# Attention and gated feed-forward in one kernel: values loaded in 128-token chunks and spread on chip, a mask by matmul in the first unit, and a new order in units 0 to 2

## The chip, the cores and the metric

The kernel runs on one core of a Trainium2 chip. The core has a matrix engine (TensorE, PE in the profile), a vector engine (VectorE, DVE), an activation engine (ScalarE, ACT), GpSimd (POOL), which here mostly issues loads, and SyncE (SP), which issues the stores of the output. Each engine runs its own instructions in program order and waits on semaphores for the others. The metric is the device time of one execution in microseconds, the median of several runs.

## The reference

There are 4 batches of 8 heads, 768 tokens, 64 numbers per head. Each query looks at the tokens less than 16 away and, through one summary key and value per block of 32 tokens, at all 24 blocks. The summary key is the maximum over the block, the summary value is its mean, and log(32) is added to the summary scores. A feed-forward stage follows:

```python
mask_l = np.abs(pos[:, None] - pos[None, :]) < window
scores_s = scale * einsum('bhsd,bhnd->bhsn', q, k_sum) + np.log(block)
a = softmax(concatenate([where(mask_l, scores_l, -1e9), scores_s]))
x = matmul(a, concatenate([v, v_sum]))          # to [3072, 512]
ffn_out = (gelu(x @ w_gate) * (x @ w_val)) @ w_out
return x + sigmoid(x @ w_res) * ffn_out
```

All inputs and the output are float32; the kernel computes in bf16 with float32 sums.

## The kernel before, in words

A unit is half a batch, 384 tokens, so there are 8 units. Within a unit the attention works in tiles of 64 queries (`QT`), six per unit, and by head pairs, four of them. The whole kernel is written out by hand under `tc.manual_schedule()`: the order of the source is the order on each engine.

**Keys.** `load_tokens` brings keys and queries to `k_sb` and `q_sb` (96 rows of consecutive tokens). `k_step` turns one head pair on PE (`turn_pair`, L204), lets ACT copy it (L211) into `kW`, lets DVE take the maximum over each block of 32 (L214) and copies the 16 neighbours on either side and the 24 block keys next to every tile (L218 to L220). So each 64-query tile has one stationary operand of 128 columns: 96 band keys and 24 block keys.

**Values.** `vext` holds for each of the 12 tiles of a batch 128 rows: 96 band values (a tile's own 64 and 16 on each side) and the block values. The band rows come straight from memory, so that tokens near a tile's border are loaded twice: by `v_tile` (L95, one tile, 8 heads) or, for tiles 1 to 5 of batch 0, by `v_head` (L101). In addition, the second half of each batch is loaded densely to `v_sb`. The block means are matmuls: `vsum_dense` and `vsum_pair` for batch 0; `vsum_grp` (L250, three groups side by side) and `vsum_place` (L257) for the others. `vsum_bc` (L263, DVE) copies the means to the last 32 rows of every tile of `vext`.

**Attention of a unit.** `s_step` computes the scores of a head pair (L273), ACT takes the exponential (L277), and DVE multiplies by the band mask (L280). `av_step` multiplies by `vext` (L296); the last column of `vext` is 1, so that it yields the denominators; DVE divides (L304, L306). `xt_step` turns the result for the feed-forward (L315, L317).

**Feed-forward of a unit.** Twelve `fo_step`s: gate and value matmuls (L328, four each), Gelu on ACT (L334), product on DVE (L335). The accumulators come from a ring of four PSUM buffers (`ps_mm`), two steps' worth. Then `res_step`, `ffn_step` and `end_step` for three groups of 128 tokens, with the attention of the next unit placed among them: this is the tail of the unit.

**Order of the work.** Before the loop over the units stands the start: keys and queries of batch 0, attention of unit 0, the first gate and value products. `turn_pair` work for the next batch stands among the `fo_step`s of the odd units; in unit 1 from step 2, in units 3 and 5 from step 0. All loads are issued by POOL in program order: keys and queries of batch 0, values, gate and value weights, `w_res`, `w_out`, then `load_batch(1)`, `load_batch(2)`, `load_batch(3)`. At most eight are in flight: each waits for the one eight places before it.

```python
def half_fo(st, w, fo, lo, hi, acc=None): acc = ps_mm.tile(...)   # L323, ring of 4
i = fo - (2 if u == 1 else 0)                                      # L420
k_step(nb, hp, *home) / q_step(q_sb[nb], nb, 0, S, hp, *home)      # L428, L430
load_batch(1)                                                      # L401
```

Of the kernel before, what the change touches and what calls it, by code (L numbers as in the profile page):

```python
# [8 lines left out]
F32 = mybir.dt.float32  # L9
# [6 lines left out]
def kernel(  # L16
# [45 lines left out]
    OWN, POST, BLK0 = WIN, WIN + QT, BAND  # L62
# [4 lines left out]
    bmat = const.tile([BAND, HT, 32], BF16, name="bmat")  # L67
    bden = const.tile([PP, 44], BF16, name="bden")
# [5 lines left out]
    place = const.tile([PP, 32], BF16, name="place")  # L74
    vpart = const.tile([128, DM], BF16, name="vpart")
# [16 lines left out]
    def v_tile(b, t):  # L92
        lo, hi = max(0, t * QT - WIN), min(S, t * QT + QT + WIN)
        r0 = lo - (t * QT - WIN)
        nc.gpsimd.dma_start(out=vext[b % 2][r0:r0 + hi - lo, t, :, 0:D],  # L95
                            in_=v[b, :, lo:hi, :].rearrange("h p d -> p h d"))

    def v_head(b, h, t0, t1):
        src = bass.AP(tensor=v.tensor, offset=v[b, h, t0 * QT - WIN:, :].offset,
                      ap=[[D, BAND], [QT * D, t1 - t0], [1, D]])  # L100
        nc.gpsimd.dma_start(out=vext[b % 2][0:BAND, t0:t1, h, 0:D], in_=src)  # L101

    k_sb, q_sb, v_sb = {}, {}, {}

    with tc.manual_schedule():

        def vext_consts(i):
            nc.vector.memset(vext[i][:, :, :, D:D + 1], 1.0)
            nc.vector.memset(vext[i][0:32, 0, :, 0:D], 0.0)
            nc.vector.memset(vext[i][64:96, NT - 1, :, 0:D], 0.0)  # L110

        def vext_edges(i):
            nc.gpsimd.affine_select(out=vext[i][0:32, 0, :, D:D + 1], in_=vext[i][0:32, 0, :, D:D + 1],
                                    compare_op=ALU.is_ge, fill=0.0, base=-WIN,
                                    pattern=[[0, H], [0, 1]], channel_multiplier=1)
            nc.gpsimd.affine_select(out=vext[i][64:96, NT - 1, :, D:D + 1],
                                    in_=vext[i][64:96, NT - 1, :, D:D + 1],
                                    compare_op=ALU.is_ge, fill=0.0, base=WIN - 1,
                                    pattern=[[0, H], [0, 1]], channel_multiplier=-1)

        def kw_consts(i):
            for p in range(NP):
                nc.vector.memset(kW[i][p][:, 0, 0:WIN], 0.0)
                nc.vector.memset(kW[i][p][:, NT - 1, POST:POST + WIN], 0.0)
                nc.vector.memset(kW[i][p][:, :, BLK0 + NB:128], 0.0)

        def own_rows(base, row, tile, block):
            nc.gpsimd.affine_select(out=bmat[:], in_=bmat[:], compare_op=ALU.is_ge, fill=0.0, base=base,
                                    pattern=[[tile, HT], [block, 32]], channel_multiplier=row)
# [4 lines left out]

        nc.vector.memset(ident[:], 0.0)
        nc.vector.memset(bias_t[:], 0.0)
        nc.vector.memset(bias_t[96:128, :], logblk)
        nc.vector.memset(maskt[:], 1.0)
        kw_consts(0)
        nc.vector.memset(bmat[:], 1.0 / BLK)  # L140
        nc.vector.memset(bden[:], 0.0)
        nc.vector.memset(bden[:, 12:24], 1.0 / BLK)
        nc.vector.memset(place[:], 0.0)
        nc.vector.memset(vsum[0][96:128, :, D:D + 1], 1.0)
# [4 lines left out]
        v_sb[0] = token_tile(TU, S, "v_sb")  # L149
# [5 lines left out]
        load_tokens(v_sb[0], v, 0, TU, S, 0, H)  # L155
        select(bias_t[96:128, :], ALU.is_ge, -30000.0, NB - 1, 0, -1)
        vext_edges(0)
        v_tile(0, 0)
        for h in range(2):
            v_head(0, h, 1, HT)  # L160
        select(maskt[0:96], ALU.is_ge, 0.0, -1, -1, 1)
        select(maskt[0:96], ALU.is_ge, 0.0, 2 * WIN - 1, 1, -1)
        own_rows(-WIN, 1, QT, -BLK)
        own_rows(BLK - 1 + WIN, -1, -QT, BLK)
        own_rows(-WIN, 1, 0, 0)
        own_rows(WIN + QT - 1, -1, 0, 0)
        select(bden[:, 12:24], ALU.is_ge, 0.0, 0, -8, 1)
        select(bden[:, 12:24], ALU.is_ge, 0.0, 7, 8, -1)
        for h in range(2, H):
            v_head(0, h, 1, HT)  # L170
        for g in range(3):
            select(place[32 * g:32 * g + 32, :], ALU.not_equal, 1.0, 6 * g, -1, 1)
        nc.vector.memset(warm[:], 0.0)
# [10 lines left out]
        for c in range(3):  # L184
            sl = slice(c * 4, (c + 1) * 4)
            nc.gpsimd.dma_start(out=w_out[:, sl], in_=wo_src[:, sl])
            v_tile(0, HT + 2 * c)
            v_tile(0, HT + 2 * c + 1)

        def load_batch(b):  # L190
            k_sb[b], q_sb[b] = token_tile(0, S, "k_sb"), token_tile(0, S, "q_sb")
            load_tokens(k_sb[b], k, b, 0, S, 0, H)
            load_tokens(q_sb[b], q, b, 0, S, 0, H)
            v_sb[b] = token_tile(TU, S, "v_sb")
            load_tokens(v_sb[b], v, b, TU, S, 0, H)
            for t in range(NT):
                v_tile(b, t)
# [10 lines left out]
        def k_step(b, hp, pool, tag):  # L208
            tp = turn_pair(k_sb[b], hp, pool, tag)
            kw = kW[b % 2][hp]  # L210
            nc.scalar.copy(kw[:, :, OWN:OWN + QT].rearrange("d t (p j) -> d t p j", j=8),  # L211
                           tp.rearrange("d j (t p) -> d t p j", t=NT))
            ks = work.tile([128, NB], BF16, tag="ks", name="ks")
            nc.vector.tensor_reduce(  # L214
                out=ks.rearrange("d (t n) -> d t n", n=2),
                in_=kw[:, :, OWN:OWN + QT].rearrange("d t (n w) -> d t n w", w=BLK),
                axis=mybir.AxisListType.X, op=ALU.max)
            nc.vector.tensor_copy(kw[:, 1:NT, 0:WIN], kw[:, 0:NT - 1, OWN + QT - WIN:OWN + QT])  # L218
            nc.vector.tensor_copy(kw[:, 0:NT - 1, POST:POST + WIN], kw[:, 1:NT, OWN:OWN + WIN])
# [7 lines left out]
        def vsum_dense(pool, tag):  # L227
            vs = pool.tile([128, DM], F32, tag=tag, name="vs")
            for j in range(4):
                nc.tensor.matmul(vs[96:128, :], bden[:, 0:32], v_sb[0][:, :, j, :],  # L230
                                 start=(j == 0), stop=False, skip_group_check=True)
            return vs

        def vsum_pair(vs, hp):
            sl = slice(hp * 128, hp * 128 + 128)
            for t in range(HT):
                nc.tensor.matmul(vs[96:128, sl], bmat[:, t, :], vext[0][0:BAND, t, 2 * hp:2 * hp + 2, 0:D],  # L237
                                 start=False, stop=(t == HT - 1), skip_group_check=True)
            nc.scalar.copy(vsum[0][96:128, 2 * hp:2 * hp + 2, 0:D],
                           vs[96:128, sl].rearrange("p (h d) -> p h d", d=D))  # L240

        def vsum_grp(b, pool, tag):
            vs = pool.tile([128, DM], F32, tag=tag, name="vs")
            for i in range(4):
                for g in range(3):
                    if g < 2 and i == 3:
                        continue
                    lhs, rhs = ((bmat[:, i, :], vext[b % 2][0:BAND, 3 * g + i, :, 0:D]) if g < 2 else
                                (bden[:, 12:44], v_sb[b][:, :, i, :]))
                    nc.tensor.matmul(vs[32 * g:32 * g + 32, :], lhs, rhs, start=(i == 0),  # L250
                                     stop=(i == (2 if g < 2 else 3)), tile_position=(0, 32 * g),
                                     skip_group_check=True)
            nc.scalar.copy(vpart[0:96, :], vs[0:96, :])

        def vsum_place(b, pool, tag):
            vs = pool.tile([128, DM], F32, tag=tag, name="vs")
            nc.tensor.matmul(vs[96:128, :], place[:], vpart[0:96, :], start=True, stop=True)  # L257
            nc.scalar.copy(vsum[b % 2][96:128, :, 0:D], vs[96:128, :].rearrange("p (h d) -> p h d", d=D))
# [6 lines left out]
        def s_step(u, hp, st):  # L265
            b, half = u // 2, u % 2
            s = ps_s.tile([128, 2, 512], F32, tag="s", name="s")
            kw, qt = kW[b % 2][hp], qT[b % 2][hp]
            for t in range(HT):
                tt = half * HT + t  # L270
                for hh in range(2):
                    ps = slice(hh * 64, hh * 64 + 64)
                    nc.tensor.matmul(s[:, hh, t * QT:(t + 1) * QT], kw[ps, tt, :],  # L273
                                     qt[ps, tt * QT:(tt + 1) * QT], start=True, stop=True,
# [4 lines left out]
            Pf = P.rearrange("p a t q -> p (a t) q")  # L279
            nc.vector.tensor_mul(Pf, Pf, maskt.unsqueeze(1).to_broadcast([128, 2 * HT, QT]))  # L280
# [90 lines left out]


        st = new_unit()
        for hp in range(NP):
            k_step(0, hp, *MM)
            q_step(qa, 0, 0, TU, hp, *MM)
            if hp:
                s_step(0, hp - 1, st)
        vs = vsum_dense(*TT)
        s_step(0, NP - 1, st)  # L380
        vsum_pair(vs, 0)
        vsum_pair(vs, 1)
        keep_warm(3)
        for hp in range(NP):
            if hp >= 2:
# [139 lines left out]
```

The softmax here doesn't subtract the row's maximum and nothing guards it: scores larger than these inputs give would overflow.

## Time and profile before

The median of three runs is 298.38 us (298.14 to 298.59). The profiled execution took 296.95 us; its span from first to last instruction is 294.9 us, and 2.05 us lie around it.

| what | us |
|---|---|
| start, to the first matmul of step 1 of unit 0 | 0 to 31.5 |
| unit 0: 12 steps, tail | to 45.85, to 67.5 |
| unit 1 (turns batch 1) | 67.5 to 103.2 |
| unit 2 | 103.2 to 133.0 |
| unit 3 (turns batch 2) | 133.0 to 168.8 |
| units 4, 5, 6 | to 198.6, 234.4, 264.1 |
| unit 7 and the last store | to 294.9 |
| PE busy | 273.0 (93%) |
| DVE, ACT busy | 164.4 (56%), 140.4 (48%) |
| POOL busy | 66.8 (23%) |

Busy time counts the instructions of an engine. Matmuls overlap one another, so that a busy PE need not be one at its peak. The line of 40 digits on the page gives the busy share of each fortieth of the span in tenths. A releaser in square brackets is what ended an engine's idle time.

### The profile page before, as it was taken

What the parts mean: (1) busy time and instruction counts of PE and PEld (TensorE: products, weight loads), DVE (VectorE), ACT (ScalarE), POOL (GpSimd) and SP (SyncE); (2) the same over time, 40 slices, a digit from 0 to 9 for tenths busy, and PEclk for the clock granted to TensorE, in tenths of its full rate; (3) what the DMA queues carried; (4) which work ended last, traced back from release to release, by engine and by line L of the source; (5) the groups of instructions that cost most, each with busy time, mean ns of one, the idle gap of its engine ahead of it and who ended that gap; (6) DMA issues with size and microseconds to landing.
All of it is one profiled execution on the core that took longest, in us unless ns stands there. A gap on an engine that the chain in (4) does not pass through costs nothing.

```text
span 294.9 us, 6313 instructions
## 1 busy us (share of the span) xinstructions
PE 273.0 (93%) x2619; PEld 151.0 (51%) x2644; DVE 164.4 (56%) x388; ACT 140.4 (48%) x218; POOL 66.8 (23%) x103
## 2 busy tenths in 40 slices
PE   1889999768998999999999999999999999999993
PEld 0655564335554556455554556455544565456541
DVE  3833551395827764486647754477647744575333
ACT  1922536704666433645656433645665434643310
POOL 8996536438346230023000000000000000000000
PEclk9999999999999999999999999999999999999999
DMA  6999999999999992019000110011000110011001
GB/s 93 172 114 186 196 198 187 195 148 204 199 136 108 215 188 20 2 37 148 4 0 2 71 38 2 2 71 38 2 0 2 71 38 1 2 71 38 0 36 71
DMA packets 58811, 24.38 MB, mean 83 GB/s; under 512 B 37536, under 2 KB 55712, under 8 KB 58784
## 3 DMA queue, kind: packets, MB, share of 16 engines
q0 software_dynamic: 55328, 17.70, 68.5%
q1 hardware_dynamic: 3456, 6.29, 6.2%
q8 instruction: 20, 0.33, 0.5%
q14 instruction: 7, 0.06, 0.1%
HBM read 35.39 MB, written 6.29 MB: 141 GB/s over the span
## 4 chain that ended last, share of the span: by engine, by line
PE 89%; DVE 4%; ACT 3%; DMA 2%; issue 1%; POOLq 0%; DVEq 0%; ACTq 0%
PE g L328 23%; PE vv L328 21%; PE f L356 20%; PE r L346 7%; PE tp L204 4%; PE ao L296 4%; PE s L273 3%; PE xp L315 2%; DMA k_sb<-in_k_dram 2%; PE vs L250 1%; DVE o L363 1%; ACT P L277 1%; DVE th L361 1%; PE wp L370 1%; PE vs L237 1%
## 5 line engine op out<-in xcount | busy, mean ns | idle before, releaser
L335 DVE TENSOR_TENSOR gvT<-ge,vv 128x384 bf16<-128x384 f32 x96 | 53.0, 553 | 61.2 <-PE vv L328 58.8
L328 PE MATMUL g<-xT,w_gate 128*128 128x384 bf16 x384 | 80.8, 328 | 1.3 <-DVE xT L317 0.8
L334 ACT ACTIVATE ge<-g 128x384 f32<-128x384 f32 x96 | 46.9, 490 | 72.0 <-DVE gvT L335 41.3
L328 PE MATMUL vv<-xT,w_val 128*128 128x384 bf16 x384 | 78.8, 328 | 0.0
L356 PE MATMUL f<-w_out,gvT 128*128 128x512 bf16 x273 | 65.7, 379 | 1.4 <-issue 0.9
L328 PEld LDWEIGHTS <-w_val 128*128 128x128 bf16 x384 | 37.6, 98 | 27.5 <-issue 3.4
L328 PEld LDWEIGHTS <-w_gate 128*128 128x128 bf16 x384 | 35.1, 98 | 24.3 <-issue 3.2
L95 POOL DMA_DIRECT2D vext<-in_v_dram x43 | 33.0, 771 | 60.7 <-PE ao L296 32.6
L277 ACT ACTIVATE P<-s,bias_t 128x768 bf16<-128x768 f32 x32 | 28.8, 901 | 29.0 <-PE s L273 28.4
L356 PEld LDWEIGHTS <-gvT 128*128 128x128 bf16 x288 | 27.0, 98 | 30.0
L280 DVE TENSOR_TENSOR P<-P,maskt 128x768 bf16<-128x768 bf16 x32 | 17.7, 554 | 21.2 <-ACT P L277 21.2
L346 PE MATMUL r<-w_res,xT 128*128 128x512 bf16 x88 | 24.2, 381 | 0.5 <-issue 0.2
L214 DVE TENSOR_REDUCE ks<-kW 128x24 bf16<-128x768 bf16 x16 | 15.2, 952 | 9.9 <-ACT kW L211 9.7
L361 DVE SCALAR_TENSOR_TENSOR th<-th,f 128x512 f32<-128x512 f32 x24 | 16.3, 679 | 7.3 <-PE f L356 7.3
L211 ACT COPY kW<-tp 128x768 bf16<-128x768 bf16 x16 | 12.8, 799 | 12.9 <-PE tp L204 12.8
L349 ACT ACTIVATE th<-r 128x512 f32<-128x512 f32 x24 | 14.3, 595 | 9.6 <-PE r L346 9.2
L306 DVE TENSOR_TENSOR xn<-ao,rz 128x384 bf16<-128x384 f32 x32 | 17.8, 557 | 1.1
L304 DVE RECIPROCAL rz<-ao 128x6 f32<-128x6 f32 x32 | 6.1, 192 | 20.3 <-PE ao L296 20.3
L296 PEld LDWEIGHTS <-P 128*64 128x64 bf16 (+2 forms) x432 | 10.7, 119 | 13.0 <-DVE P L280 5.1
L224 ACT COPY qT<-tp 128x768 bf16<-128x768 bf16 (+1 forms) x20 | 13.5, 673 | 8.0 <-PE tp L204 8.0
L363 DVE SCALAR_TENSOR_TENSOR o<-th,xn 128x512 f32<-128x512 f32 x24 | 16.6, 692 | 0.8
L204 PE MATMUL tp<-ident,k_sb 96*64 96x96 bf16 x256 | 9.8, 227 | 6.4 <-DMA k_sb<-in_k_dram 6.4
(70 smaller groups left out, 199.6 us busy)
## 6 DMA issues: line engine op xcount, KB each, us to landing
out_dram<-o SPq DMA_DIRECT2D x24, 256.0 KB, 2.3
vext<-in_v_dram POOLq DMA_DIRECT2D x35, 96.0 KB, 8.5
k_sb<-in_k_dram POOLq DMA_DIRECT2D x3, 768.0 KB, 10.7
q_sb<-in_q_dram POOLq DMA_DIRECT2D x3, 768.0 KB, 13.7
v_sb<-in_v_dram POOLq DMA_DIRECT2D x4, 384.0 KB, 15.1
w_gate<-in_moe_w_gate_dram POOLq DMA_DIRECT2D x6, 256.0 KB, 8.6
w_val<-in_moe_w_val_dram POOLq DMA_DIRECT2D x6, 256.0 KB, 9.2
w_out<-in_moe_w_out_dram POOLq DMA_DIRECT2D x3, 512.0 KB, 14.5
```

The costliest lines, as they stand in the source:

```text
L95: nc.gpsimd.dma_start(out=vext[b % 2][r0:r0 + hi - lo, t, :, 0:D], in_=v[b, :, lo:hi, :].rearrange("h p d -> p h d"))
L204: nc.tensor.transpose(tp[hh * 64:hh * 64 + 64, j, :], src[:, 2 * hp + hh, j, :], ident[0:PP, 0:PP])
L277: nc.scalar.activation(P.rearrange("p a t q -> p a (t q)"), s[:, :, 0:TU], AF.Exp, scale=scale, bias=bias_t[:])
L296: nc.tensor.matmul(ao[64 * e:64 * e + 64, sub, hh, :], P[rows, hh, t, :], rhs, start=blocks is None or (not blocks and sub == 0 and hh == ...
L306: nc.vector.tensor_mul(xn, ao[:, :, :, 0:D], rz.to_broadcast([128, NSUB, 2, D]))
L328: nc.tensor.matmul(acc[:, 0:TU], w[:, ko, fs], st["xT"][:, ko, :], start=(ko == 0), stop=(ko == KO - 1))
L334: nc.scalar.activation(ge[:], g[:, 0:TU], AF.Gelu)
L335: nc.vector.tensor_mul(gvT[:, fo, :], ge[:], vv[:, 0:TU])
L346: nc.tensor.matmul(r[:], st["xT"][:, ko, ss], w_res[:, ko, :], start=(ko == 0), stop=(ko == KO - 1))
L356: nc.tensor.matmul(st["f", sub][:], gvT[:, fo, ss], w_out[:, fo, :], start=(fo == 0), stop=(fo == FO - 1))
L361: nc.vector.scalar_tensor_tensor(th[:], th[:], 1.0, f[:], ALU.add, ALU.mult)
L363: nc.vector.scalar_tensor_tensor(o[:], th[:], 0.5, st["xn"][:, sub, :], ALU.mult, ALU.add)
```

## The change

1. **Loads of values.** One `load_values` per 128 tokens writes the even tile of `vext` (128 rows); `v_tile`, `v_head` and `v_sb` are gone. The band rows are stored in another order: own 64 first, then the 16 after, then the 16 before (`POST`, `PRE`), and `kW` likewise.
2. **Spreading.** `v_spread` on DVE copies from the even tiles what the odd tiles need, and the borders: for each half of a batch five copies and one `memset`. It stands in the start and in unit 0 step 0 (batch 0), in unit 1 step 9 and unit 2 step 0 (batch 1), in unit 2 step 4 and unit 4 step 0 (batch 2), in unit 4 step 4 and unit 6 step 0 (batch 3).
3. **Block means.** Six matmuls of 512 columns over the even tiles (`vsum_sum`) and one copy replace `vsum_grp` and `vsum_place`; `vsum_bc` runs in halves of a batch, two calls per step.
4. **Keys.** The block maximum is a `tensor_max` of two halves and a reduce of half the size.
5. **First scores.** In unit 0 the mask is added by two matmuls per head pair (`ident` by `nmask`); the DVE multiplication is left out there.
6. **Start.** Ten matmuls on a zero tile before the first keys, more of them between the steps; the tables for Exp and Gelu are asked for early by one-element activations; av over the band for all head pairs first, then the block part.
7. **Order.** The tail of unit 0 is written anew. In unit 1 the turning starts at step 0. `load_batch(b + 2)` stands at the start of odd units. `load_batch(1)` stands twice in a row.

```diff
+        def load_values(b, c):
+            nc.gpsimd.dma_start(out=vext[b % 2][:, 2 * c, :, 0:D],
+                                in_=v[b, :, c * 128:(c + 1) * 128, :].rearrange("h p d -> p h d"))
...
         def load_batch(b):
             k_sb[b], q_sb[b] = token_tile(0, S, "k_sb"), token_tile(0, S, "q_sb")
             load_tokens(k_sb[b], k, b, 0, S, 0, H)
             load_tokens(q_sb[b], q, b, 0, S, 0, H)
-            v_sb[b] = token_tile(TU, S, "v_sb")
-            load_tokens(v_sb[b], v, b, TU, S, 0, H)
-            for t in range(NT):
-                v_tile(b, t)
+            for c in range(NT // 2):
+                load_values(b, c)
...
+            km = work.tile([128, NT, 2, BLK // 2], BF16, tag="km", name="km")
+            nc.vector.tensor_max(km[:], own[:, :, :, 0:BLK // 2], own[:, :, :, BLK // 2:BLK])
...
+        def vsum_sum(b, pool, tag, chunks=range(NT // 2), vs=None):
...
+            for c in chunks:
+                lo = NB - 4 - 4 * c
+                nc.tensor.matmul(vs[96:128, :], bmean[:, lo:lo + 32], vext[b % 2][:, 2 * c, :, 0:D],
+                                 start=(c == 0), stop=(c == NT // 2 - 1), skip_group_check=True)
...
+        def v_spread(b, c0, c1):
+            V = vext[b % 2].rearrange("p (c e) h d -> p c e h d", e=2)
+            last = NT // 2
+            copy = nc.vector.tensor_copy
+            copy(V[0:64, c0:c1, 1, :, 0:D], V[64:128, c0:c1, 0, :, 0:D])
+            copy(V[64:96, c0:c1, 1, :, 0:D], V[32:64, c0:c1, 0, :, 0:D])
+            if c0 == 0:
+                nc.vector.memset(V[64:96, 0, 0, :, 0:D], 0.0)
+            lo = max(c0, 1)
+            copy(V[64:96, lo:c1, 0, :, 0:D], V[32:64, lo - 1:c1 - 1, 1, :, 0:D])
+            copy(V[64:80, c0:c1, 0, :, 0:D], V[0:16, c0:c1, 1, :, 0:D])
+            hi = min(c1, last - 1)
+            copy(V[64:80, c0:hi, 1, :, 0:D], V[0:16, c0 + 1:hi + 1, 0, :, 0:D])
+            if c1 == last:
+                nc.vector.memset(V[64:80, last - 1, 1, :, 0:D], 0.0)
...
+            if first:
+                for hh in range(2):
+                    nc.tensor.matmul(s[:, hh, 0:TU].rearrange("p (t q) -> p t q", t=HT), ident[:],
+                                     nmask.unsqueeze(1).to_broadcast([128, HT, QT]),
+                                     start=True, stop=False, skip_group_check=True)
...
+        def values_step(u, fo):
+            b = u // 2 + 1
+            first = 8 if u == 1 else 3
+            if (u == 1 or u in (2, 4)) and fo >= first:
+                nb = 1 if u == 1 else b
+                if fo == first:
+                    vs = vsum_sum(nb, *SS)
+                    vsum_out(nb, vs, 0, H, nc.scalar.copy)
+                if fo == first + 1:
+                    v_spread(nb, 0, HT // 2)
+                if first + 1 < fo < first + 4:
+                    vsum_bc(nb, 2 * (fo - first - 2), 0, HT)
+                    vsum_bc(nb, 2 * (fo - first - 2) + 1, 0, HT)
+            if u % 2 == 0 and u < NU - 1:
+                if fo == 0:
+                    v_spread(b - 1, HT // 2, NT // 2)
+                if fo in (1, 2):
+                    vsum_bc(b - 1, 2 * (fo - 1), HT, NT)
+                    vsum_bc(b - 1, 2 * (fo - 1) + 1, HT, NT)
...
+        load_batch(1)
         load_batch(1)
 
         for u in range(NU):
...
-            if half == 0 and 1 < nb < B:
-                load_batch(nb)
+            if half == 1 and b + 2 < B:
+                load_batch(b + 2)
...
+                if half == 1 and nb < B and fo < 8:
+                    hp, kq = (fo % NP, fo // NP) if u == 1 else (fo // 2, fo % 2)
...
+                s_step(n, 0, nst)
+                res_step(st, 0)
+                s_step(n, 1, nst)
+                res_step(st, 1)
+                s_step(n, 2, nst)
+                av_step(n, 0, nst)
+                res_step(st, 2)
+                s_step(n, 3, nst)
...
```

## The prediction

> **What bounds the kernel now.** I read the page's chain that ended last first, then the busy digits, then the loads with their landings, then PE and DVE in order of time around unit 1.
>
> ```profile
> PE 89%; DVE 4%; ACT 3%; DMA 2%; issue 1%; POOLq 0%; DVEq 0%; ACTq 0%
> DMA  6999999999999992019000110011000110011001
> k_sb<-in_k_dram POOLq DMA_DIRECT2D x1, 768.0 KB, 11.3
> 71.02 0.53 PE L204 MATMUL tp<-ident,k_sb 96*64 96x96 bf16 x16
> 28.98 1.17 PE L328 MATMUL vv<-xT,w_val 128*128 128x384 bf16 x3
> 31.50 0.81 PE L328 MATMUL g<-xT,w_gate 128*128 128x384 bf16 x4
> L263 DVE COPY vext<-vsum 32x1536 bf16<-32x1536 bf16 x12 | 6.8, 607 | 0.5 <-ACT vsum L258 0.3
> L109 DVE MEMSET vext<- 32x512 bf16 x2 | 1.0, 485 | 0.0
> L335 DVE TENSOR_TENSOR gvT<-ge,vv 128x384 bf16<-128x384 f32 x96 | 53.0, 553 | 61.2 <-PE vv L328 58.8
> ```
>
> PE carries 89% of the chain. The DMA digits are 9 without a gap to about 110 us. Batch 1's keys were issued at 46.69 and landed 11.3 us later, at 58.0; PE first needs them at 71.02. So 13 us of slack lie there, inside a stretch where the DMA engines have none. The two L328 pieces show the array's speed: three matmuls of 384 columns advance 0.96 us at 28.98 (0.32 to 0.35 each), while four take 0.65 us from 31.5 on (0.163). DVE's product (0.55 us) fills under half of a step of 1.30 us; the rest is its room.
>
> **What the Trainium skill says.** "TensorE: Matmul & The Clock Gate", Part 1: the array starts at half rate, reaches full rate after about 3.4 us of sustained work and falls back after an idle window of that length. The trace agrees: half speed until 31.3 us, though the granted clock reads 1.00. "VectorE: DVE Perf Modes", the perf-mode tier table: bf16 copies within SBUF can run at four elements a cycle. The 1536-element copies of L263 (0.607 us mean, pairs in 1.04) agree. The same page, "Two Vector instructions with no wait between them": an instruction whose start quadrant differs from its predecessor's starts only when that has finished; no row of before isolates this. "DMA: Bandwidth & Descriptors", "Issuing engines are not separate DMA queues": all loads and stores share the same 16 engines. The stores of unit 0 at 62 to 67 us stand beside slower loads here.
>
> **Loads, from their landings.** Batch 0's keys and queries are down at 10.95; unchanged. Six value chunks of 128 KB: heads and tiles of values (128 B rows) moved 480 KB from 14.1 to 18.4 us (112 KB/us) and about 98 KB/us at 83 to 95 us, so a chunk is 1.15 to 1.3, say 1.25 us, and the values are down at 18.5 (before: 18.4). Twelve weight chunks, 20.4 to 36.6 us for eleven intervals with one hiccup, 1.33 to 1.47 each: 35.2. The second queries 2.05, `w_res` 2.55, three `w_out` at 2.75: 48.0 (before 52.8, since six value tiles lay between). Then `load_batch(1)` twice. Keys and queries of a batch take 3.43 each (54.6 to 58.0 to 61.45). First copy: 51.5, 54.9, values 62.4. Second copy, the one that `k_step` reads, since the second call replaces the tile: keys 65.8. Unit 0's three stores, 0.8 us each (6.2% of the span for 24), fall into this: 68.3. Counting from the old landing of batch 1's queries instead (61.45 + 2.3 for more 128 B rows + 3.4 keys + 2.5 stores) gives 69.6; the bytes ahead are otherwise nearly equal. I take **68.7**, with 65.5 to 71 as ends. The POOL queue does not delay it: each load waits for the one eight before, and behind it are only later loads. Second queries are due at about 72, values at 80, both before their use.
>
> **PE's arrival there.** Exponentials of unit 0 end near 17 either way; the last values that the first half needs land at about 16, `v_spread` (3.15, below) ends at 19.2, four band av with warm-up matmuls 3.0, then four DVE divisions of 0.76 and turning, 6: the loop starts near 28 (before 31.5). Twelve steps 14.3, plus 1.9 for the second `v_spread`: 44. The tail held 14.7 us of PE work in 21.7; with one table load (1.28) and the chain of exponentials still in it I put 17: 61, and one step: **62.5**. PE then stands about 6 us at `k_step(1, 0)`. Everything gained in the start and in unit 0 (weights, `nmask`'s eight matmuls at 0.16 to 0.35, warm-up, tables, `tensor_max`: 0.36 + 0.55 for 0.95) is therefore costed at nothing: the wait for the second keys hides it. Without that cover it would show as up to 6 us.
>
> **Sum.**
> - *Arrival.* In before, turning starts at 70.95 with steps 0 to 2 done; after, with step 0 only done. Two steps are 2.60, so the equal point is 68.35. Against 68.7: **+0.35**.
> - *Cold array.* After 6 us idle the next 3.4 us or more run at half rate: **+2.0** (0 if PE waits under 3.4, 3 at most).
> - *`v_spread`.* Four copies of 1536 elements at 0.55, one of 1024 at 0.42, one memset 0.485: 3.1, with waits between quadrants 3.15 us. It stands on DVE ahead of the next step's product, whose accumulator PE needs two steps later. Unit 2, step 0: the first product is late already (105.38, 2.15 us after the unit's first matmul), ends at 2.7; the spread to 5.9; product 1 to 6.45; PE wants the buffer at 4.7: 1.8 lost. Two pairs of `vsum_bc` (0.36 each) keep DVE behind; the second spread in step 4 costs PE 1.2 more. With the means (six matmuls at 0.216: 1.3) unit 2 grows by 4.3; unit 4 likewise; unit 6 (one spread, no means) by 1.9.
> - *Unit 1.* Plain steps and tail as in unit 2, 29.75, plus eight turns at 0.565 and the means 1.3; the spread of step 9 delays the product that frees `ffn_step`'s buffer by 0.7: 36.27 against 35.71, +0.56. Its four `k_step`s in a row fit DVE as before: 1.78 of 1.87 us a step.
> - *Units 3 and 5.* No means, no broadcasts: 34.27 against 35.79, −1.5 each.
> - Units 1 to 6: 0.56 + 4.3 + 4.3 + 1.9 − 3.0 = **+8.1**. Unit 7 is unchanged.
>
> Together 0.35 + 2.0 + 8.1 = +10.4: the span goes from 294.9 to 305.3, the profiled execution from 296.95 to 307.4. The median lay 1.43 above that execution, so 298.38 + 10.4 = **308.8**. Moving `load_batch(2)` and `(3)` earlier costs nothing: they were hidden by 30 us or more.
>
> **Rivals.**
> *A, the second load is early, and decides the sign.* If the second keys land by the time PE comes, the change is (landing − 68.35) + 8.1 with no cold stretch. Should the start end at 25 and PE reach `k_step` at 59, and the keys land there too, it is −9.4 + 8.1: 297.1, faster. It decides at a landing of 60.25. For it: rates of 230 GB/s on keys. Against it: 2.3 MB more in a stretch of full digits. At 62.5 it gives +2.2, 300.6. Chance 0.15, half of it faster or equal.
> *B, the copies run slower.* Sources in `v_spread` are strided where L263's are broadcasts; at two elements a cycle a copy is 0.96, a spread 5.0, and units 2, 4, 6 lose 1.85 per spread, unit 1 too: 11 more, 320; at one element a cycle (1.76 a copy) 342. For it: no row shows this form. Against: same row length and destination. 0.09.
> *C, the room absorbs the spread.* If PE's ring gives more slack than two steps, the stalls go (3.0 in units 2 and 4, 1.9 in unit 6, 0.7 in unit 1, together 8.6) and +1.8 remains: 300.2. Against it: in unit 2's first eight steps DVE has 13.7 us of work (eight products 4.5, two spreads 6.3, eight broadcasts 2.9) and PE 11.7. 0.08.
> *Main*: 0.68.
>
> **How the numbers follow.** The predicted time is the main case. Its own range: landing −3 to +2, cold −2 to +1, spread at 2.8 to 3.6 us ∓2.5: 303 to 313.5. The range to hold 8 in 10 reaches down to A's slow half and C, 300, and up to 314.5; A's faster half and B stay out. About 0.2% (0.6 us) is what a measurement of this kernel can tell from none. Faster 0.06 (A), same 0.03 (A near 60), slower 0.91.
>
> **What would show it.** Right: a PE wait of 4 to 8 us at the turning of `k_sb` in unit 1, released by DMA; matmuls of 384 columns at twice their time for some us after; keys issued twice; gate-and-value waits of 1 to 2 us on DVE twice in units 2 and 4, once in unit 6; units 3 and 5 shorter by 1.5; copies of 1536 at 0.55. Wrong: no wait at that turning, or a landing before 61; spreads that cost PE nothing; copies above 0.9 us; a start that ends later than 35, so that PE, not the load, comes last.

## The result and the profile after

The changed kernel takes **302.88 us** (300.75 to 303.24, four runs) against 298.26 (298.11 to 298.59, four runs) for the kernel before: **1.014 times** the time, 95% interval 1.009 to 1.019. Ratios here and below are of the means, without runs more than 1.5% above the fastest of their kernel. So it is slower, by 4.6 us in the median, where 10.4 were forecast. The profiled execution took 303.24 us with a span of 301.5, the slowest of the four, against 296.95 and 294.9 before. The spans therefore differ by 6.6, more than the medians; the stages below add up to 6.6. Each border is the first gate matmul of a unit; only the start, and unit 0 of the kernel before, end at the last matmul of step 0's gate.

| stage (us) | before | after | difference | forecast |
|---|---|---|---|---|
| start, to the last matmul of step 0's gate | 31.04 | 34.83 | +3.8 | −3.5, hidden |
| unit 0 | 36.5 | 35.1 | −1.3 | −3, hidden |
| unit 1 | 35.7 | 36.65 | +0.9 | +0.56, and +2.35 for a late load |
| unit 2 | 29.75 | 32.5 | +2.7 | +4.3 |
| unit 3 | 35.8 | 34.3 | −1.5 | −1.5 |
| unit 4 | 29.75 | 32.55 | +2.8 | +4.3 |
| unit 5 | 35.8 | 34.3 | −1.5 | −1.5 |
| unit 6 | 29.75 | 30.5 | +0.75 | +1.9 |
| unit 7 | 30.8 | 30.8 | 0 | 0 |

From the page of the changed kernel: the chain that ended last by engine; the digits of granted clock and of DMA; and from the listing of POOL in order of time the issue of batch 2's keys.

```profile
PE 78%; DVE 13%; issue 3%; ACT 2%; DMA 2%; POOL 0%; DVEq 0%; POOLq 0%
PEclk9586799999999999999999999999999999999999
DMA  6999999999997190009000110001000100010001
63.49 0.79 POOL L86 DMA_DIRECT2D k_sb<-in_k_dram  x1 [2.24 <-DMA k_sb<-in_k_dram]
```

DVE's share of the chain has grown from 4% to 13%. The clock digits 5, 8, 6, 7 stand in the first 38 us. The last line tells when the second copy of batch 1's keys is down: this load waited for it until just before 63.49. The copy was issued at 50.00 and took 13.2 us to landing, so it landed at 63.2. The forecast was 68.7. PE in order of time, around unit 1 (start, duration, engine, line, operation):

```profile
69.97 0.81 PE L302 MATMUL g<-xT,w_gate 128*128 128x384 bf16 x4
70.61 0.81 PE L302 MATMUL vv<-xT,w_val 128*128 128x384 bf16 x4
71.36 0.53 PE L174 MATMUL tp<-ident,k_sb 96*64 96x96 bf16 x16
71.82 0.82 PE L302 MATMUL g<-xT,w_gate 128*128 128x384 bf16 x4
```

The turning of the keys at 71.36 has no releaser: PE comes 8 us after the load. The matmuls after it advance 0.66 us per four, full speed. So neither the wait nor the cold array of the forecast exists in this profile; the loss is elsewhere. Two places show it. First the start, PE alone:

```profile
20.89 0.19 PE L270 MATMUL ao<-vext,P 96*64 96x65 bf16 x1 [2.35 <-DVE vext L222]
21.49 0.49 PE L270 MATMUL ao<-vext,P 96*64 96x65 bf16 x11 [0.41 <-DVE vext L224]
21.91 1.03 PE L344 MATMUL wp<-warm 128*128 128x512 bf16 x2
22.87 0.54 PE L270 MATMUL ao<-vext,P 96*64 96x65 bf16 x12
23.35 1.04 PE L344 MATMUL wp<-warm 128*128 128x512 bf16 x2
...
26.23 1.03 PE L344 MATMUL wp<-warm 128*128 128x512 bf16 x2
27.19 0.93 PE L203 MATMUL vs<-vext,bmean 128*32 128x512 bf16 x2
```

PE waits 2.35 us for `v_spread`, and then does four av parts of 12 small matmuls each (0.54), with two warm-up matmuls after every one (L344: 1.03 for two, half rate). From 21.49 to 27.19 there is work for PE alone, and two thirds of it is warm-up. Second, the steps of unit 2, PE and DVE together:

```profile
116.31 0.70 DVE L216 COPY vext<-vext 64x1536 bf16<-64x1536 bf16 x1
117.04 0.69 DVE L217 COPY vext<-vext 32x1536 bf16<-32x1536 bf16 x1
...
119.21 0.68 DVE L224 COPY vext<-vext 16x1536 bf16<-16x1536 bf16 x1
119.92 0.56 DVE L309 TENSOR_TENSOR gvT<-ge,vv 128x384 bf16<-128x384 f32 x1
120.52 0.81 PE L302 MATMUL vv<-xT,w_val 128*128 128x384 bf16 x4 [0.68 <-DVE gvT L309]
```

A spread takes 3.6 us (forecast 3.15). While it runs, PE does steps 6, 7 and the gate of 8, and waits only 0.68 us, at the value matmuls of step 8, for the product of step 5: three steps of room, where the prediction had two. The times tell why: the gate of step 8 starts at 119.03, just after the Gelu of step 7 (118.49 to 118.98) has read the gate before it. So a gate's buffer is free again early, and the values of steps 5, 6 and 7 can wait in the other three of the four. The groups of after by form, busy time and mean of one (ns), that answer those shown of before:

```profile
L231 DVE COPY vext<-vsum 32x768 bf16<-32x768 bf16 x28 | 9.3, 375 | 0.4
L216 DVE COPY vext<-vext 64x1536 bf16<-64x1536 bf16 x8 | 5.7, 718 | 0.3
L217 DVE COPY vext<-vext 32x1536 bf16<-32x1536 bf16 x8 | 5.6, 695 | 0.2
L219 DVE MEMSET vext<- 32x512 bf16 x4 | 1.9, 485 | 0.2
```

The copies of 1536 elements within `vext` take 0.68 to 0.72 us on average, between the 0.55 of the main case and the 0.96 of rival B; the `memset` is as before.

### The profile page after: what moved, and what is told of

It reads as the page before. It is cut to its first block, busy times and chain, and to the rows that moved or that the text cites. A ratio compares the mean times of both kernels' runs of the same rounds, so it can differ in the third digit from the quotient of the medians.

```text
span 301.5 us, 6317 instructions
## 1 busy us (share of the span) xinstructions
PE 279.2 (93%) x2609; PEld 149.9 (50%) x2634; DVE 189.7 (63%) x462; ACT 138.7 (46%) x214; POOL 50.6 (17%) x71
## 4 chain that ended last, share of the span: by engine, by line
PE 78%; DVE 13%; issue 3%; ACT 2%; DMA 2%; POOL 0%; DVEq 0%; POOLq 0%
PE f L330 19%; PE g L302 18%; PE vv L302 17%; PE r L320 7%; PE tp L174 5%; PE ao L270 4%; DVE gvT L309 3%; PE s L246 3%; PE xp L289 2%; PE wp L344 2%; PE vs L203 2%; DMA q_sb<-in_q_dram 2%; DVE vext L216 1%; DVE vext L231 1%; DVE vext L217 1%
## 5 line engine op out<-in xcount | busy, mean ns | idle before, releaser
L309 DVE TENSOR_TENSOR gvT<-ge,vv 128x384 bf16<-128x384 f32 x96 | 52.2, 552 | 38.8 <-PE vv L302 35.8
L302 PEld LDWEIGHTS <-w_gate 128*128 128x128 bf16 x384 | 35.2, 98 | 25.9 <-issue 5.0
L92 POOL DMA_DIRECT2D vext<-in_v_dram x30 | 26.6, 892 | 60.8 <-PE xp L289 30.1
L254 DVE TENSOR_TENSOR P<-P,maskt 128x768 bf16<-128x768 bf16 x28 | 15.6, 556 | 18.3 <-ACT P L250 18.2
L270 PEld LDWEIGHTS <-P 128*64 128x64 bf16 (+2 forms) x432 | 10.4, 114 | 19.1 <-issue 8.7
L270 PE MATMUL ao<-vext,P 128*64 128x65 bf16 (+1 forms) x384 | 13.0, 205 | 5.0 <-DVE vext L222 2.3
L195 ACT COPY qT<-tp 128x768 bf16<-128x768 bf16 (+1 forms) x20 | 13.2, 672 | 8.2 <-PE tp L174 8.2
L246 PE MATMUL s<-qT,kW 64*128 64x64 bf16 x384 | 11.4, 194 | 1.6 <-ACT P L250 1.5
```

The source lines that it names most:

```text
L92: nc.gpsimd.dma_start(out=vext[b % 2][:, 2 * c, :, 0:D], in_=v[b, :, c * 128:(c + 1) * 128, :].rearrange("h p d -> p h d"))
L270: nc.tensor.matmul(ao[64 * e:64 * e + 64, sub, hh, :], P[rows, hh, t, :], rhs, start=blocks is None or (not blocks and sub == 0 and hh == ...
L302: nc.tensor.matmul(acc[:, 0:TU], w[:, ko, fs], st["xT"][:, ko, :], start=(ko == 0), stop=(ko == KO - 1))
L309: nc.vector.tensor_mul(gvT[:, fo, :], ge[:], vv[:, 0:TU])
```

## Experiments

Theory after this reading: two losses, the spreads in one block on DVE and the warm-up matmuls in PE's order in the start; the second load costs nothing because PE comes later than it. Rivals: the load counts after all; the warm-ups keep the array fast and the start is slow for another reason. All times are medians; the ratio is to the kernel before on the same chip (298.1 in the first and third group, 297.8 in the second).

**The second load, once and three times.**

```diff
         load_batch(1)
-        load_batch(1)
```

> The changed kernel with load_batch(1) once. Theory (the second load is wholly hidden, the changed kernel lost its time in the start and at the spreads): the turning of batch 1 in unit 1 still starts at about 71.4 us, unit times as in the changed kernel, median 302.9 within 1 us. Rival (the 2.3 MB of the second load delay w_out, the second queries or PE in unit 0): unit 0 gets shorter and the median falls by 2 us or more.

301.75 us (298.73 to 303.22, 12 runs), ratio 1.012 [1.008, 1.015]. The interval overlaps that of the changed kernel (1.009 to 1.019), and the turning starts at 71.06, close to 71.36: no cost can be seen, though one of about 1 us is not excluded.

```diff
         load_batch(1)
         load_batch(1)
+        load_batch(1)
```

> The changed kernel with load_batch(1) three times, so that the keys that PE reads land one more batch later. Theory (a copy costs nothing until its keys land after PE comes, at 71.4 us): the keys land at 63.2 + 3.8 + 6.8 + 3.4, about 77.5 us, with the stores of unit 0 near 80; PE waits about 6 us at the first turning in unit 1, then runs at half speed for some 3 us: median 308 to 312. Rival (the DMA engines have room, extra loads never reach PE): 303.

312.18 us (311.16 to 313.98), ratio 1.049 [1.044, 1.054]. PE in order of time:

```profile
66.18 0.81 PE L302 MATMUL vv<-xT,w_val 128*128 128x384 bf16 x4
78.05 0.85 PE L174 MATMUL tp<-ident,k_sb 96*64 96x96 bf16 x16 [11.05 <-DMA k_sb<-in_k_dram]
78.83 1.46 PE L302 MATMUL g<-xT,w_gate 128*128 128x384 bf16 x4
80.08 1.43 PE L302 MATMUL vv<-xT,w_val 128*128 128x384 bf16 x4
81.45 0.53 PE L174 MATMUL tp<-ident,k_sb 96*64 96x96 bf16 x16
81.91 0.82 PE L302 MATMUL g<-xT,w_gate 128*128 128x384 bf16 x4
```

Here is all that the forecast saw, one load later: a wait at this very turning, released by DMA, and half rate after it. The landing came as expected; the wait is longer because in this execution PE came at 67.0. The cold stretch costs 1.5 us: 3.40 from one turning to the next at 78.05, 1.86 at the one after. So the wait comes once the keys land after PE has come; in the changed kernel they land 8 us before.

**The warm-ups of the start.** Those between the head pairs stand in two loops: keys and scores ("pairs"), and the band av.

```diff
             if hp:
                 s_step(0, hp - 1, st, True)
-            keep_warm(2)
...
             av_part(0, hp, st, *(MM if hp else AO), blocks=False)
-            keep_warm(2)
```

> The changed kernel without the warm-up matmuls between the steps of the start (the ten at the very beginning stay). Theory (they run on a half-speed array and stand in the way of the keys' turning, so that the start ends at 34.8 instead of 31.3): the start ends at 29 to 31 us, median 298 to 300. Rival (they keep the array at full speed for what follows, and the start is bound by the vector engine's spread): the start ends no earlier than 34, median 303 or more.

297.21 us (296.52 to 299.08, 20 runs), ratio 0.9985 [0.997, 1.000]: 5.7 us less than the changed kernel, more than expected, and level with the kernel before. The loop is reached at 29.31 instead of 34.83. The kernel before is no start without warm-ups, though: it has seven of its own, three ahead of the first av and two each after the second and third pair (L370 at 18.80, 22.40 and 24.95 us). What it would gain without them was not run. With only the second of the two lines taken out:

> The changed kernel without the warm-up matmuls after each head pair of the band av; those between the head pairs of keys and scores stay. Theory: the four pairs in the av part are the loss, since there PE waits for nothing else (21.5 to 27.2 us in the changed kernel against 20.15 to 21.1 without them), and those between keys and scores bring something, as they did in the kernel before: 295 to 297.5. Rival, that both groups cost alike: 299 to 300.

297.33 us (296.63 to 299.46, 20 runs), ratio 1.000 [0.998, 1.002]. The whole loss of the warm-ups is that of the four pairs in the av part: 5.5 us against the changed kernel (four runs), 4.4 against its form with one load (301.75, 12 runs). Those between keys and scores neither bring nor cost anything here, so that half of the expectation fell. PE:

```profile
19.91 1.48 PE L270 MATMUL ao<-vext,P 96*64 96x65 bf16 x47 [0.55 <-DVE vext L224]
21.32 1.04 PE L203 MATMUL vs<-vext,bmean 128*32 128x512 bf16 x2
...
29.55 0.32 PE L302 MATMUL g<-xT,w_gate 128*128 128x384 bf16 x1 [0.57 <-ACT xT L291]
```

The stretch from the av matmuls to the means takes 1.41 us where it took 5.70, and it too is at half rate: eight matmuls of 512 columns did not buy a faster array for the av matmuls, they only stood in front. The loop starts 5.3 us earlier; 4.3 of this is the stretch; ahead of it 1.6 come from matmuls that the changed kernel ran at half rate from 7.9 to 14 us, and behind it 0.6 are lost again. Without any warm-up, the ten at the beginning left out too:

> The changed kernel without any warm-up matmul, the ten at the beginning left out too. If the ten bring nothing once the others are gone: the same as without those between, 297.2 +- 0.7. If they are what makes the array fast from 17 us on: the start ends 1 to 3 us later, 298.5 to 300.

297.77 us (296.62 to 299.64, 12 runs), ratio 1.000 [0.998, 1.002], level with the run that kept the ten: a gain from them cannot be told from none. And the other way round, in the kernel before, two after each head pair of keys and scores:

```diff
+        nc.vector.memset(warm[:], 0.0)
...
-        nc.vector.memset(warm[:], 0.0)
...
                 s_step(0, hp - 1, st)
+            keep_warm(2)
         vs = vsum_dense(*TT)
```

> The kernel before with two warm-up matmuls after every head pair of the start, eight in all, and nothing else. Theory that warm-ups stand in PE's way between the head pairs: at half rate eight take about 3.8 us, of which PE's idle time there covers some 1 us, so +2 to +4, 300 to 302. Rival, that they only harm together with the new start (masking matmuls, spread): within 0.7 of 298.1.

294.57 us (293.08 to 297.6, four runs), ratio 0.987 [0.984, 0.991] from the three fastest: faster, against the theory, on few runs that lie far apart. So a warm-up is not bad as such; why these gain is not shown. The profile of this kernel fell on its slowest execution (297.6, loop at 30.66), so where the other three gain isn't seen; in this one the array is at full rate at 19.73, where the kernel before is at half rate (the same 12 av matmuls, 0.38 against 0.54; this run first, then the kernel before):

```profile
19.73 0.38 PE L296 MATMUL ao<-vext,P 96*64 96x65 bf16 x12
```

```profile
19.79 0.54 PE L296 MATMUL ao<-vext,P 96*64 96x65 bf16 x12
```

**The spread.** One copy or `memset` per step instead of six in a row; in addition the means and first halves of batches 2 and 3 stand in units 3 and 5.

```diff
-                if fo == first + 1:
-                    v_spread(nb, 0, HT // 2)
+                at = (3, 4, 5, 6, 7, 8, 9) if u == 1 else (0, 1, 3, 5, 7, 8, 9)
+                if fo == at[0]:
+                    vs = vsum_sum(b, *SS)
+                    vsum_out(b, vs, 0, H, nc.scalar.copy)
+                elif fo in at:
+                    spread_ops(b, 0, HT // 2)[at.index(fo) - 1]()
...
-                if fo == 0:
-                    v_spread(b - 1, HT // 2, NT // 2)
+                if fo < 6:
+                    spread_ops(b - 1, HT // 2, NT // 2)[fo]()
+                elif fo < 10:
+                    vsum_bc(b - 1, fo - 6, HT, NT)
```

> The changed kernel with the six parts of each spread put one per gate-and-value step (batches 2 and 3: first half and means moved from units 2 and 4 to units 3 and 5). Theory (a spread costs PE only by standing in one piece ahead of a product; one copy of 0.7 and one product of 0.55 fit into a step of 1.30): no wait of PE for a product in units 2, 4 and 6; unit 2 and 4 near 29.8 to 30.3, unit 6 near 29.8, units 3 and 5 near 35.7; median 1.5 to 2.5 us below the changed kernel, about 300.7. Rival (the vector engine's total work is the bound): as the changed kernel.

295.78 us (294.35 to 296.52, seven runs), ratio 0.993 [0.991, 0.996], much more than expected. The span from the loop's start to the end is 260.9 us against 266.7: −5.8, of which unit 0 −2.1, units 2, 4 and 6 −2.7, −2.8 and −0.75 (each is back at the 29.75 of the kernel before), unit 1 −0.3, and units 3 and 5 +1.4 each for the means. The expectation had left out unit 0, whose second spread was in one block too. DVE and PE in unit 2:

```profile
110.43 0.56 DVE L313 TENSOR_TENSOR gvT<-ge,vv 128x384 bf16<-128x384 f32 x1
110.81 0.81 PE L306 MATMUL vv<-xT,w_val 128*128 128x384 bf16 x4
111.15 0.48 DVE L225 MEMSET vext<- 16x512 bf16 x1 [0.16 <-issue]
111.46 0.81 PE L306 MATMUL g<-xT,w_gate 128*128 128x384 bf16 x4
111.73 0.55 DVE L313 TENSOR_TENSOR gvT<-ge,vv 128x384 bf16<-128x384 f32 x1
112.11 0.81 PE L306 MATMUL vv<-xT,w_val 128*128 128x384 bf16 x4
```

Between two products there is one piece of the spread, and PE's four advance 0.65 us without a wait. The same copies cost nothing in this form, which also shows that it was their standing in a row, not DVE's total, that cost. The rest of the gain is in the start, which this edit leaves alone but which reaches the loop at 32.72 in this profile; the section on the prediction comes back to such scatter.

To measure the room, each spread inside the loop was made twice in a row:

```diff
                     v_spread(nb, 0, HT // 2)
+                    v_spread(nb, 0, HT // 2)
...
                     v_spread(b - 1, HT // 2, NT // 2)
+                    v_spread(b - 1, HT // 2, NT // 2)
```

> The changed kernel with each spread inside units 1, 2, 4 and 6 made twice in a row; the second pass copies rows that the first one has overwritten, so its values are not those of the reference. Each spread grows from 3.65 to 7.3 us. With three steps of room for the product, the first spread of units 2 and 4 (no wait now, about 0.9 us of room) costs about 2.8, the second 3.6 more, that of unit 6 3.6 more, unit 1's at most 3.6 more: +13 to +20, 316 to 322. With two steps of room as the prediction had it the same growth would be at the full 3.65 each: +22 to +26, 325 to 329.

334.2 us (332.75 and 335.65), ratio 1.122 [1.116, 1.128]: above both expectations, and the edit did more than the expectation counted, since it doubled unit 0's spread as well. PE at the first and second spread of unit 2 and at that of unit 6:

```profile
122.61 0.81 PE L302 MATMUL vv<-xT,w_val 128*128 128x384 bf16 x4 [2.63 <-DVE gvT L309]
133.40 1.44 PE L302 MATMUL vv<-xT,w_val 128*128 128x384 bf16 x4 [5.25 <-DVE gvT L309]
274.87 0.92 PE L302 MATMUL vv<-xT,w_val 128*128 128x384 bf16 x4 [4.07 <-DVE gvT L309]
```

The first wait is 2.63 (three steps of room: 2.8), that of unit 6 4.07 (0.42 and 3.65 make 4.07). In sum, though, units 1, 2, 4 and 6 grow by 5.7, 9.9, 8.8 and 5.3, unit 0 by 4.4. What the expectation left out is visible in the second line: after a wait of 5.25 us the next four matmuls take 1.44 instead of 0.81, and the granted clock stays at 0.50 from about 132 to 138 us. So a wait has two prices here: its length, and after those of 4.07 and 5.25 us, not after that of 2.63, the array's rate.

**Everything put together.** One load, no warm-ups between the head pairs, one copy per step:

> The second load of batch 1 taken out, no warm-up matmuls between the head pairs of the start, and the spread one copy per step with the means of batches 2 and 3 in units 3 and 5. If the losses found one by one add up: the loop over the units begins near 29.3 as without warm-ups, units 0 to 7 take 260.9 as with one copy per step, span 290.2, time 292.1 +- 1. If the gain of one copy per step came from a luckier clock in the start: 296 to 297.

291.24 us (291.11 to 291.64, five runs), ratio 0.978 [0.976, 0.981]. The losses add up; units 0 to 7 take 260.0 us. This version is **faster than both kernels**, 6.5 us below the one before. Against the run without warm-ups between (297.21) it also gives the price of the spreads with the load: 6.0 us. The mask by matmul was undone on top of it:

```diff
-                s_step(0, hp - 1, st, True)
+                s_step(0, hp - 1, st)
```

(and the same for the last head pair)

> The combined kernel with the first scores masked by DVE again, the eight masking matmuls left out. The prediction costed this part at nothing. If PE bounds the pairs of the start, eight matmuls of 0.16 to 0.41 us are saved and DVE's four products of about 0.9 us have room: 289.5 to 291.2. If DVE bounds them, the spread starts later behind the products: 292 to 294.

293.19 us (292.63 to 293.54), ratio 0.984 [0.981, 0.987]: 1.95 us more, 1.7 by the ratios. The second expectation held in its time, but DVE is not full: what binds is its order. DVE in order of time, with the product:

```profile
17.44 0.56 DVE L258 TENSOR_TENSOR P<-P,maskt 128x768 bf16<-128x768 bf16 x1 [1.70 <-ACT P L254]
18.03 0.88 DVE L217 COPY vext<-vext 64x1536 bf16<-64x1536 bf16 x1
```

and without it:

```profile
15.98 0.70 DVE L217 COPY vext<-vext 64x1536 bf16<-64x1536 bf16 x1
```

The spread waits behind the last product, which leaves DVE idle for 1.70 us until the last exponential, and starts 2.05 us later. Lastly six warm-ups where PE waits anyway, ahead of the first av:

```diff
         v_spread(0, 0, HT // 2)
+        keep_warm(6)
```

> The same as the combined kernel with six warm-up matmuls in PE's order just before the first av, where PE waits about 1.7 to 2.3 us for the spread. Theory that the clock falls back because a stretch of about 3.4 us is mostly idle: the array stays at full rate through part of 20 to 31 us and the start gets 1 to 3 us shorter, 289.5 to 291.5. Rival, that only the queue position of a warm-up matters and this one is free: same as the combined kernel within 0.5 us.

290.23 us (289.36 to 291.18, five runs), ratio **0.9745** [0.972, 0.977], the fastest version, about 1 us below the combined kernel. The intervals overlap, but four of these five runs lie below all five of that kernel. PE:

```profile
17.74 1.47 PE L348 MATMUL wp<-warm 128*128 128x512 bf16 x6
19.39 0.19 PE L274 MATMUL ao<-vext,P 96*64 96x65 bf16 x1 [0.18 <-DVE vext L222]
20.15 0.93 PE L274 MATMUL ao<-vext,P 96*64 96x65 bf16 x47 [0.57 <-DVE vext L223]
```

The warm-ups fill the wait to its last 0.18 us, and the av matmuls after them take 0.86 us to the means instead of 1.41 in the combined kernel. With the pairs' warm-ups put back in addition:

> The combined kernel with six warm-up matmuls in the wait for the spread, and again two after each head pair of keys and scores. If those bring the 3 us that they brought in the kernel before: 287 to 289. If the six in the wait already give what there is to be had: 290.2 +- 0.7.

291.46 us (288.76 to 292.81, six runs), ratio 0.977 [0.973, 0.982]: wider, not better.

## Why the prediction was wrong

The direction and the range held; the size was less than half, and it came about in another place than the forecast had it. In the spans 6.6 us came for 10.4: start and unit 0 gave 2.45 where arrival and cold array were to give 2.35, and units 1 to 6 gave 4.2 for 8.1. So nearly the whole difference in size is in the `v_spread` term, while the mechanism failed at the arrival. Of the other 2.0, between the spans and the medians, 1.7 is that the profiled execution of before lay 1.3 below its median and this one 0.4 above.

- ***PE's arrival there*** is the step that failed first, and two other steps rested on it. The start was to end at 28 and PE to come at 62.5; it ended at 34.83 and PE came at 71.36. The step counted "four band av with warm-up matmuls 3.0"; they took 5.70, and without the warm-ups 1.41. They stood in PE's order ahead of av matmuls that were ready, so that PE did them first. That is 2.7 of the 6.8 us by which the start was late; the spread ended at 21.4 instead of 19.2, after pairs partly at half rate, and from the means on the start took 7.6 for 6. Unit 0's steps then took 16.7 for 16, its tail 18.4 for 17. The prediction had named this sign, a start later than 35, "so that PE, not the load, comes last"; 34.83 is at its edge. Rival A had the order right, keys down before PE comes, but expected it of an early load; its sum, with PE's 71.36 put in, has +3.0 for the arrival.
- ***The landing*** (68.7, ends 65.5 to 71) was 63.2, below its range. The weights were down at 33.4 instead of 35.2, the values at 60.0 instead of 62.4. And the three stores, put ahead of the keys at 2.5 us, were issued at 67.99, after the keys, because unit 0's tail, which was to end at 61, ended at 69.97.
- ***Arrival*** (+0.35) and ***Cold array*** (+2.0) therefore did not occur. That start and unit 0 together cost nearly the sum of the two is chance. Both mechanisms are real: with a third load the wait comes, and the cold stretch costs 1.5, so that its size was only a little off.
- *"Everything gained in the start … is costed at nothing"* lost its cover: 4.4 to 5.5 us of warm-ups became visible, and the mask by matmul, counted at nothing, gives 1.7 to 2 (measured in the combined kernel).
- ***`v_spread`*** had the right mechanism and a wrong size. The copies were sized too short (0.55 where 0.70 came, a spread 3.15 where 3.6 came), and the room too: the value accumulator is wanted three steps after the product, not "two steps later". Unit 2's +2.7 is 1.42 of means, 0.68 of wait, and 0.6 that is mostly steps of 1.40 us instead of 1.30; the forecast had 1.3 and 3.0. Rival C, that the ring gives more than two steps, was right in this; at 300.2 it erred in that it had the stalls go altogether (units 1 to 6 at −0.5, where 4.2 came).
- ***Units 3 and 5***, −1.5 each, held, and unit 1 at +0.56 too: of the +0.9 in the table about 0.5 is three gate matmuls that the kernel before does ahead of the border at 67.5.

By the runs, the changed kernel pays 4.4 to 5.5 us for warm-ups in the av part and about 6 for spreads in blocks, and has by difference some 6 to 7 us of gains on the other side, which leaves the +4.6. Among these are unit 0's tail (18.4 for 21.7), the mask and units 3 and 5; they were not taken apart further.

"TensorE: Matmul & The Clock Gate", Part 1 of the Trainium skill says that the clock follows a free-running window of about 3.4 us, so that the same kernel counts a different number of cold matmuls from run to run. The runs agree. The prediction used the page only for the cold stretch and not for the scatter of the start that it implies: five kernels with the same start reach the loop at 34.83 (changed kernel), 34.13 (one load), 32.72 (one copy per step), 30.97 (three loads) and 30.34 (spread twice). So what two single profiles differ by in the start is not the worth of an edit; the medians are.

The prediction's "The trace agrees", of the 3.4 us of sustained work, was read too quickly. In the kernel before PE is busy 7.78 of the 8 us from 22 to 30 and stays at half rate until 31.3.

## What to carry to other kernels

By these runs a warm-up matmul belongs where its engine waits in any case; in the av part, ahead of ready work, eight cost their full time at half rate. That eight between the pairs gained in the kernel before is an open end. Before costing an edit at nothing because a wait hides it, forecast that wait from both sides, since here both the load and the engine moved and the cover was gone. Work put on a half-idle engine costs by the length of its longest unbroken piece against the room of the ring behind it: the spreads as blocks of six cost about 6 us in all, the same copies one per step none.

## What was not expected of the hardware

The granted clock in the start of the changed kernel, from stretches of 0.5 us, switches at about 7.40, 14.22, 21.05, 27.88, 31.29 and 34.70 us: 6.82, 6.83, 6.83, 3.41 and 3.41 apart, each one or two times 3.41. In four-us stretches (PE, PEld, DVE, ACT and POOL busy with their counts, then the granted clock, the DMA share, GB/s):

```profile
8.00:12.00 4.00, 3.78 (x41) 1.64 (x42) 2.80 (x9) 2.32 (x4) 3.93 (x7) 0.50 1.90 174
16.00:20.00 4.00, 2.38 (x32) 1.05 (x33) 3.55 (x9) 2.85 (x5) 2.77 (x5) 1.00 1.47 195
24.00:28.00 4.00, 3.64 (x30) 1.20 (x30) 0.00 (x0) 0.00 (x0) 2.28 (x3) 0.52 1.45 197
```

PE is busy in the two cold stretches (8 to 12 and 24 to 28 us) and less so in the fast one between them, just before the array falls back at 21.05: by these figures it falls for what PE did before. Why it then stays at half rate for twice 3.41 us while PE works is not shown. The array fell to half rate at 7.40, though PE had worked up to 4.95 and again from 6.43: a gap of 1.5 us with 0.5 more behind it was enough here, less than the idle window of 3.4 us that the prediction took from the page. In two kernels with the same start (three loads, one copy per step) the ten warm-ups ended at 5.6 to 5.8, and the array stayed fast until 19 to 20 us. Their end alone does not decide. In the run without warm-ups between, the same up to there, they ended at 5.78 too, and the turning after them is at half rate (0.85 for 16, against 0.53):

```profile
6.42 0.85 PE L174 MATMUL tp<-ident,k_sb 96*64 96x96 bf16 x16 [0.64 <-DMA k_sb<-in_k_dram]
```

There PE is busy without a break from 9 to 17 us and still at half rate. So neither a short gap nor steady work is enough to tell the rate; that the position of the window decides is argued from these intervals, not shown.
